# Block means as four narrow products side by side, first transposes of a pair in score banks, first weight pieces in halves, and other places for the first attention steps

## The chip, the cores and the metric

The kernel runs on one core of a Trainium2 chip, in one launch. The metric is the device time of that launch in microseconds (us), the median of three runs. TensorE (PE) does the matrix products, VectorE (DVE) and ScalarE (ACT) the work on elements, GpSimd (POOL) some copies, SyncE (SP) issues the loads.

## The reference

Sparse attention over 4 batches x 8 heads x 768 tokens x 64 numbers, then a gated network without a nonlinearity. Each query sees the keys less than 16 tokens away, and one summary for each of the 24 blocks of 32 tokens: the largest key by component, the mean value.

```python
k_sum = k.reshape(B, H, nb, block, D).max(axis=3)
v_sum = v.reshape(B, H, nb, block, D).mean(axis=3)
scores_l = scale * np.matmul(q, k.transpose(0, 1, 3, 2))
scores_s = scale * np.einsum('bhsd,bhnd->bhsn', q, k_sum) + np.log(block)
scores_l_m = np.where(np.abs(pos[:, None] - pos[None, :]) < window, scores_l, -1e9)
a = softmax(np.concatenate([scores_l_m, scores_s], axis=-1))
x = np.matmul(a, np.concatenate([v, v_sum], axis=2))   # heads side by side: 3072 x 512
out = ((x @ w1) * (x @ w2) @ w3) @ w_out               # 512 -> 1024 -> 1024 -> 512
```

## The kernel before

The 3072 tokens are done in six units of 512. In a unit the heads are taken two at a time: one step (a *pair*, four in a unit) fills the 128 rows of `x` that these two heads own. A pair is a chain: scores on PE (`scores`, L310, tile `sc`), mask and row maximum on DVE (`reduce`, L328), exponentials on ACT (`expose`, L344), the sum's reciprocal (`invert`, L351: an addition on POOL, then DVE), the scaling by it (`normalize_alone`, L358, on DVE or ACT as the string `NORMALIZE` says), transposes on PE (`transposes`, L366, tile `tp`) into two PSUM banks, copies to SBUF (`evacuate`, L376, the second on the engine that `SECOND` names), the products with the values (`outputs`, L385, tile `po`) and `keep_x` (L402).

`w3` and `w_out` are first multiplied into one 1024 x 512 matrix `wp` (`fold_weights`, L193), so that a unit needs `x @ w1`, `x @ w2`, their product (`gate`, L412) and one product with `wp` (`project`, L444). Every product of the weights is three single-pass products of a high and a low part. The weights come as eight-byte numbers in pieces of 512 columns (`wraw`), and `convert` (L152) makes the two parts of each: a pass on ACT (L167), a shift and an OR on DVE (L175, L178), a rounding copy on ACT (L188, the high part) and a subtraction on DVE (L109, the low part). The pieces, the four raw key tiles and the three value tiles of the first batch, and the network's `h` tiles share a ring of ten buffers.

The order on SP and PE is the order in which the code is written; DVE, ACT and POOL are ordered by the scheduler, except in `SOONER` parts that go ahead. Until the first eight pairs are done, a loop over steps `t` (L641) writes that order: each step starts one weight piece, and the tables `LOADS` (by pieces issued) and `WORK` (by step) say after which one a load or a piece of work is put. `FIRST` names the step at which each of the eight pairs begins, and `RATE` and `LATER_RATE` say how many columns of products of the weights go on PE between two steps. `EARLY` is the order of the first pieces, `EARLY_PRODUCTS` that of the first products.

The means of the first batch's values are products too: `mean_products` (L257) multiplies a 128 x 120 matrix of 1/32 and 0 by the 512 columns of each of six blocks of 128 tokens, and one ACT copy takes the result to `vs`. Later batches use sums on DVE (L247).

The banks: `mm` and `tp` have two each, `sc` has four. The accumulators of the third and fourth row block of the fold take the two `tp` banks until `store` (L209) has read them.

Of the kernel before, what the change touches and what calls it, by code (L numbers as in the profile page):

```python
# [15 lines left out]
ALU = mybir.AluOpType  # L16
# [14 lines left out]
FIRST = (15, 18, 20, 22, 27, 32, 37, 44)  # L31
# [4 lines left out]
    *(("wo", 0, 0), ("w3", 0, 0), ("wo", 0, 1), ("w3", 1, 0), ("wo", 1), ("w3", 2, 0), ("w3", 3, 0)),  # L36
    *(("w3", 0, 1), ("w3", 1, 1), ("wo", 2), ("w3", 2, 1), ("w3", 3, 1), ("wo", 3)),
# [10 lines left out]
NORMALIZE = "VAAAAAAA"  # L48
SECOND = "AAAVAVVA"
# [21 lines left out]
def attention_moe(ctx, tc, qG, kW, kT, vP, vW, vB, mask, w1, w2, w3T, wo, out):  # L71
# [23 lines left out]
    ident = const.tile([P, P], F32, name="ident")  # L95
    make_identity(nc, ident)
    mask_sb = const.tile([P, 3, KR], F32, name="mask_sb")


    mean_sb = sb.tile([P, S // P, P], F32, name="mean_sb", tag="v", bufs=2)  # L100
    nc.gpsimd.memset(mean_sb, 0.0)
    for i in range(P // BLOCK):
        for at in (CUT, CUT - 64):
            part = mean_sb.rearrange("p t n -> p (t n)")[i * BLOCK : (i + 1) * BLOCK, at + i :: P + P // BLOCK]
            nc.gpsimd.memset(part[:, : S // P], 1.0 / BLOCK)
# [22 lines left out]
    def weight(name, i, src, shape, part=None):  # L128

        n = src.shape[1] // 2  # L130
        parts = range(n // PIECE) if part is None else [part]
        units.append((name, i, shape, list(parts), len(todo) + len(parts) - 1))
        for k in parts:
            todo.append(src[:, 2 * k * PIECE : 2 * (k + 1) * PIECE])

    def start_loads(at_least):

        while todo or due_loads:
# [8 lines left out]
            nc.sync.dma_start(raw, todo.pop(0))  # L147
# [4 lines left out]
    def convert(name, i, shape, parts, last):  # L152


        n = len(parts) * PIECE
# [6 lines left out]
        for k in range(len(parts)):  # L162
# [3 lines left out]
            low_words.append(words[:, :, 0])  # L166
            nc.scalar.activation(  # L167
                f[:, k * PIECE : (k + 1) * PIECE],
# [7 lines left out]
        for k, low_word in enumerate(low_words):  # L176
            some = bits[:, k * PIECE : (k + 1) * PIECE]
# [8 lines left out]
        at = parts[0] * PIECE  # L186
# [4 lines left out]
        have.update((name, i, part) for part in parts)  # L191

    def fold_weights(order):  # L193
        acc = {}
        for i, j in order:
            while not {("w3", i, j * P // PIECE), ("wo", j // 2, j % 2 * DO // PIECE)} <= have:
# [88 lines left out]
    def load_sums(u, p, v):  # L285
        for b, blocks, n in batches(u):
            for g, at in enumerate((CUT, CUT - 64)):
# [4 lines left out]
                else:  # L292
                    src = vs[b][at : at + NB, p * P : (p + 1) * P]
# [64 lines left out]
    def normalize_alone(s, sm, mx):  # L358

        if NORMALIZE[s] == "A":  # L360
            for j in range(NI):
                nc.scalar.activation(sm[:, j], sm[:, j], AF.Copy, scale=mx[:, 2, j : j + 1])
        else:
            nc.vector.tensor_tensor(sm, sm, mx[:, 2].unsqueeze(2).broadcast_to([P, NI, KR]), ALU.mult)
# [47 lines left out]
    def gate(f, x, hs):  # L412
        acc = []
        for w in range(2):
# [6 lines left out]
            for c in range(NC):  # L421
                while (GATES[w], k, c * FQ // PIECE) not in have:
# [46 lines left out]
    def queue(name, i, part=None):  # L469
        src, shape = {"wo": (wo, (2, DO)), "w3": (w3T, (NJ, P)), "w1": (w1, (NC, FQ)), "w2": (w2, (NC, FQ))}[name]  # L470
        weight(name, i, src[i], shape, part)
# [83 lines left out]
    def first_pair(s):  # L555
# [13 lines left out]
        pt = evacuate(transposes(sms.pop(s)[0]), SECOND[s])  # L569
# [20 lines left out]
    def means():  # L590
        po = mean_products(vraws)
        vraws.clear()
        vs[0] = sb.tile([KR, DM], F32, name="vs0", tag="pt", bufs=6)
# [181 lines left out]
```

## Time and profile before

| what | value |
|---|---|
| median of 3 runs (lowest, highest) | 539.33 us (539.18, 541.11) |
| the profiled execution: its own time, its span | 540.83 us, 539.0 us |
[...]
| busy: PE, weight loads, DVE, ACT, POOL | 517.9, 421.8, 237.5, 238.9, 56.3 us |
| moved by DMA | 67.21 MB, mean 125 GB/s |

The span is the time from the first to the last instruction; the execution's own time is 1.83 us longer. The first 90 us are the fold of the weights and the first pairs, the rest is the network with the later pairs between its products. Names such as `mm<-w,w` read: tile written, then tiles read; x12 is the count. The products of scores, means and values stand as two records each, a transpose as one.

### The profile page before, as it was taken

Reading aid. Unit: us, or ns where it says so; the run is one execution under the profiler, and the core shown is the slowest. Engines: PE = TensorE matmul, PEld = TensorE weight load, DVE = VectorE, ACT = ScalarE, POOL = GpSimd, SP = SyncE. Lnnn points to the kernel's source line nnn. Section 1 sums busy time; section 2 is a strip of 40 time slices with the busy share of each in tenths; the row PEclk is TensorE's granted clock in tenths of the full one; section 3 lists DMA queues with packets and bytes.
Section 4 is the critical chain, followed back from the end, with each engine's and each line's share of the span. In section 5 each row is a group of like instructions: output and inputs, shape, how many; then the busy total and the mean of one; then the engine's idle time right before and its main releaser. Section 6 shows DMA issues by size and latency. Waiting matters only on the chain.

```text
span 539.0 us, 9912 instructions
## 1 busy us (share of the span) xinstructions
PE 517.9 (96%) x3852; PEld 421.8 (78%) x3852; DVE 237.5 (44%) x686; ACT 238.9 (44%) x688; POOL 56.3 (10%) x103
## 2 busy tenths in 40 slices
PE   2897999999999999999999999999999999999997
PEld 1655777888788888888888888888888888888885
DVE  5868889999503226724244033252042351122210
ACT  5547898887345225226235144253162261222210
POOL 1001221111001101103003002011021020000000
PEclk9988899999999999999999999999999999999999
DMA  8999689956524005544032141050160020000001
GB/s 309 403 348 350 189 270 369 280 183 197 167 96 154 0 1 169 162 128 135 0 111 60 40 152 58 0 157 33 40 190 1 1 75 39 21 21 0 1 19 58
DMA packets 30574, 67.21 MB, mean 125 GB/s; under 512 B 4032, under 2 KB 7616, under 8 KB 30528
## 3 DMA queue, kind: packets, MB, share of 16 engines
q1 hardware_dynamic: 27072, 60.30, 35.2%
q10 hardware_dynamic: 3456, 6.29, 3.1%
q8 instruction: 30, 0.49, 0.4%
q14 instruction: 16, 0.13, 0.1%
HBM read 58.51 MB, written 6.29 MB: 120 GB/s over the span
## 4 chain that ended last, share of the span: by engine, by line
PE 91%; DVE 3%; ACT 3%; DMA 1%; issue 1%; POOL 0%; SPq 0%; POOLq 0%; ACTq 0%
PE mm L113 79%; PE po L393 5%; PE sc L319 4%; PE tp L373 2%; DVE w L109 1%; DMA wraw<-in_w3T_dram 1%; DVE wf L178 1%; ACT w L188 1%; PE means L260 1%; ACT sm L347 1%; DVE wf L175 1%; ACT wf L167 0%; ACT wp L211 0%; DVE wp L109 0%; POOL k L306 0%
## 5 line engine op out<-in xcount | busy, mean ns | idle before, releaser
L113 PE MATMUL mm<-x,w 128*128 128x512 f32 x1152 | 264.9, 390 | 0.0
L113 PEld LDWEIGHTS mm<-x,w 128*128 128x128 f32 x1152 | 215.4, 188 | 45.6 <-issue 0.5
L113 PE MATMUL mm<-wp,h 128*128 128x512 f32 x576 | 133.9, 391 | 0.0
L113 PEld LDWEIGHTS mm<-wp,h 128*128 128x128 f32 x576 | 107.5, 188 | 22.7 <-issue 0.2
L347 ACT ACTIVATE sm<-sm,mx 128x120 f32<-128x120 f32 x192 | 73.6, 387 | 19.9 <-DVE mx L333 19.9
L438 DVE TENSOR_TENSOR g<-mm,g 128x512 f32<-128x512 f32 x48 | 33.1, 689 | 90.6 <-PE mm L113 88.7
L439 ACT CAST h<-g 128x512 fp32r<-128x512 f32 x48 | 29.6, 618 | 87.7 <-DVE g L438 87.7
L113 PE MATMUL mm<-w,w 128*128 128x512 f32 x192 | 54.1, 435 | 12.6 <-ACT w L188 11.5
L113 PEld LDWEIGHTS mm<-w,w 128*128 128x128 f32 x192 | 38.2, 206 | 25.6 <-ACT w L188 13.3
L457 ACT COPY o<-mm 128x512 f32<-128x512 f32 x24 | 14.1, 585 | 81.3 <-PE mm L113 81.3
L109 DVE TENSOR_TENSOR h<-g,h 128x512 fp32r<-128x512 f32 x48 | 35.7, 743 | 24.2 <-ACT h L439 24.0
L435 ACT COPY g<-mm 128x512 f32<-128x512 f32 x48 | 28.0, 584 | 35.6 <-PE mm L113 35.2
L333 DVE CUSTOM_DVE_ANT_0 sm<-sc,mask_sb 128x120 f32<-128x120 f32 x192 | 41.0, 275 | 5.5 <-PE sc L319 5.5
L382 DVE COPY pt<-tp 120x512 f32<-120x512 f32 x19 | 12.4, 686 | 67.7 <-PE tp L373 67.7
L306 POOL COPY k<-ks 128x96 f32<-128x96 f32 (+1 forms) x32 | 10.1, 327 | 252.3 <-DMA k<-in_kW_dram 210.0
L347 ACT ACTIVATION_READ_ACCUMULATOR sm<-sm,mx 128x1 f32 x192 | 36.5, 190 | 0.0
L109 DVE TENSOR_TENSOR x<-po,x 128x512 fp32r<-128x512 f32 x24 | 16.6, 690 | 42.2 <-ACT x L404 42.2
L356 POOL TENSOR_TENSOR sm<-sm,mx 128x960 f32<-128x960 f32 x16 | 29.1, 1820 | 6.0 <-DVE mx L353 5.0
L167 ACT ACTIVATE wf<-wraw 128x512 f32<-128x512 f32 x40 | 26.1, 669 | 6.2 <-DMA wraw<-in_wo_dram 2.7
L188 ACT CAST w<-wf 128x1024 fp32r<-128x1024 f32 (+1 forms) x25 | 21.9, 875 | 12.8 <-DVE wf L178 12.7
L393 PEld LDWEIGHTS po<-pt,v 120*64 120x64 f32 x768 | 23.8, 138 | 4.7 <-issue 2.9
L109 DVE TENSOR_TENSOR w<-wf,w 128x1024 fp32r<-128x1024 f32 (+1 forms) x25 | 25.4, 1014 | 4.4 <-ACT w L188 4.1
(33 smaller groups left out, 281.1 us busy)
## 6 DMA issues: line engine op xcount, KB each, us to landing
k<-in_kW_dram SPq DMA_DIRECT2D x24, 368.0 KB
wraw<-in_w3T_dram SPq DMA_DIRECT2D x16, 512.0 KB
wraw<-in_w_dram SPq DMA_DIRECT2D x16, 512.0 KB
q<-in_qG_dram SPq DMA_DIRECT2D x24, 256.0 KB
raw<-in_kT_dram SPq DMA_DIRECT2D x16, 384.0 KB
out_dram<-o ACTq DMA_DIRECT2D x24, 256.0 KB
v<-in_vW_dram SPq DMA_DIRECT2D x24, 192.0 KB
raw<-in_vB_dram SPq DMA_DIRECT2D x12, 384.0 KB
```

The source lines that it names most:

```text
L109: eng.tensor_tensor(dst, src, hi.bitcast(F32), ALU.subtract)
L113: nc.tensor.matmul(acc, lhsT=a, rhs=b, start=first and i == 0, stop=last and i == len(terms) - 1)
L167: nc.scalar.activation(f[:, k * PIECE : (k + 1) * PIECE], words[:, :, 1].bitcast(F32), AF.Prelu, scale=2.0**-112, alpha=-(2.0**32),)
L188: nc.scalar.copy(hi, f)
L319: nc.tensor.matmul(sc[h][64 * g : 64 * g + 64, i * KR : (i + 1) * KR], lhsT=q[rows, i * P + 64 * g : i * P + 64 * g + 64], rhs=k[rows, i, ...
L333: nc.vector.tensor_tensor_reduce(out=sm[:, j], in0=sc[h][:, i * KR : (i + 1) * KR], in1=mask_sb[:, 0 if blk == 0 else 2 if blk == BLOCKS - ...
L347: nc.scalar.activation(sm[:, j], sm[:, j], AF.Exp, bias=mx[:, 0, j : j + 1], scale=-1.0, accum_out=mx[:, 1, j : j + 1])
L356: nc.gpsimd.tensor_tensor(sm, sm, mx[:, 2].unsqueeze(2).broadcast_to([P, NI, KR]), ALU.mult)
L393: nc.tensor.matmul(po[cols, at : at + 64], lhsT=v[:, g, i, cols], rhs=pt[g][:, (h * NBLK + i) * 64 : (h * NBLK + i + 1) * 64], start=True, ...
L435: nc.scalar.copy(g, a[:, :U])
L438: nc.vector.tensor_tensor(g, acc[1][:, :U], g, ALU.mult)
L439: nc.scalar.copy(h[:, 0], g)
```

## The change

Five edits, all in the first part of the program.

1. `mean_products` uses a 128 x 24 matrix and does each of the six blocks as four products of 128 columns, one for each pair of heads, each into its own 32 partitions of one bank; four ACT copies follow, and `load_sums` reads its pair from there. The matrix has a buffer of its own and no longer takes one of the two `v` buffers.
2. `BANKS`: the transposes of the first pair go into two of the four `sc` banks.
3. The first two pieces of `wo` and `w3` come as two halves of 256 columns each, in turn.
4. `NORMALIZE` and `SECOND` change: the scaling is done once on POOL, three times on DVE and four times on ACT (once on DVE and seven times on ACT before); the second copy is on DVE once instead of three times. `store` goes ahead (`SOONER`).
5. `FIRST`, `LOADS`, `WORK`, `RATE` and `LATER_RATE` have other numbers.

```diff
-FIRST = (15, 18, 20, 22, 27, 32, 37, 44)
+FIRST = (16, 20, 22, 25, 31, 37, 41, 44)
-    *(("wo", 0, 0), ("w3", 0, 0), ("wo", 0, 1), ("w3", 1, 0), ("wo", 1), ("w3", 2, 0), ("w3", 3, 0)),
+    *(("wo", 0, 0, 256), ("w3", 0, 0, 256), ("wo", 0, 256, 256), ("w3", 0, 256, 256), ("wo", 0, 512)),
+    *(("w3", 1, 0), ("wo", 1), ("w3", 2, 0), ("w3", 3, 0), ("w3", 0, 512), ("w3", 1, 512), ("wo", 2)),
...
-NORMALIZE = "VAAAAAAA"
-SECOND = "AAAVAVVA"
+NORMALIZE = "PVAVAVAA"
+SECOND = "AAAAVAAA"
+BANKS = "STTTTTTT"
...
-                nc.scalar.copy(wp[i][:, 0], done)
-                low(nc.vector, wp[i][:, 1], done, wp[i][:, 0])
+                with tc.high_priority(offset=SOONER):
+                    nc.scalar.copy(wp[i][:, 0], done)
+                    low(nc.vector, wp[i][:, 1], done, wp[i][:, 0])
...
         po = ps.tile([P, 512], F32, name="means", tag="sc", bufs=4)
         for i in range(S // P):
-            nc.tensor.matmul(
-                po[:KR, :DM],
-                lhsT=mean_sb[:, i, :KR],
-                rhs=tiles[i // 2][:, i % 2],
-                start=i == 0,
-                stop=i == S // P - 1,
-            )
-        return po
+            for p in range(NPAIR):
+                nc.tensor.matmul(
+                    po[32 * p : 32 * p + NB, :P],
+                    lhsT=mean_sb[:, i],
+                    rhs=tiles[i // 2][:, i % 2, p * P : (p + 1) * P],
+                    start=i == 0,
+                    stop=i == S // P - 1,
+                )
+        yield
+        vs[0] = sb.tile([P, P], F32, name="vs0", tag="pt", bufs=6)
+        for p in range(NPAIR):
+            nc.scalar.copy(vs[0][32 * p : 32 * p + NB], po[32 * p : 32 * p + NB, :P])
...
+            eng = nc.vector if NORMALIZE[s] == "V" else nc.gpsimd
+            eng.tensor_tensor(sm, sm, mx[:, 2].unsqueeze(2).broadcast_to([P, NI, KR]), ALU.mult)
...
-        pt = evacuate(transposes(sms.pop(s)[0]), SECOND[s])
+        pt = evacuate(transposes(sms.pop(s)[0], **(SPARE if BANKS[s] == "S" else {})), SECOND[s])
...
-        11: [lambda: fetch(0)],
+        10: [lambda: rows(1), lambda: fetch(0)],
...
-    RATE = 6600
-    LATER_RATE = 6944
+    RATE = 5000
+    LATER_RATE = 7544
```

The order on PE around the means, before (w_253 is the third tile of `wo`, w_357 the fourth, w_115, w_137, w_171 and w_196 the first four of `w3`, w_106 the first of `wo`, w_415 the fifth of `w3`):

```order
L113 MATMUL mm<-w_253,w_171 128x512 x6
L260 MATMUL means<-rows,mean_sb 120x512 x6
L113 MATMUL mm<-w_253,w_196 128x512 x6
L319 MATMUL sc<-k,q 64x120 x16
L113 MATMUL mm<-w_357,w_115 128x512 x6
L113 MATMUL mm<-w_357,w_137 128x512 x6
L113 MATMUL mm<-w_357,w_171 128x512 x6
L113 MATMUL mm<-w_357,w_196 128x512 x6
L373 MATMUL tp<-ident,sm 120x64 x16
L319 MATMUL sc<-k,q 64x120 x16
L113 MATMUL mm<-w_106,w_415 128x512 x6
```

and now (w_274 and w_395 are the third and fourth of `wo`; w_111, w_148, w_191, w_214 the first four of `w3`):

```order
L115 MATMUL mm<-w_274,w_191 128x512 x6
L267 MATMUL means<-rows,mean_sb 24x128 x24
L329 MATMUL sc<-k,q 64x120 x16
L115 MATMUL mm<-w_274,w_214 128x512 x6
L115 MATMUL mm<-w_395,w_111 128x512 x6
L115 MATMUL mm<-w_395,w_148 128x512 x6
L115 MATMUL mm<-w_395,w_191 128x512 x6
L115 MATMUL mm<-w_395,w_214 128x512 x6
L386 MATMUL tp<-ident,sm 120x64 x16
L329 MATMUL sc<-k,q 64x120 x16
L115 MATMUL mm<-w_102,w_436 128x512 x6
```

The scores of the first pair stand ahead of six products now, and thirty products stand between them and their transposes, where it was twenty-four.

The loads on SP's queue up to the third tile of `wo`, before (wraw_164 and wraw_185 are its two pieces):

```order
L147 DMA wraw_142<-in_w3T_dram 128x1024
L254 DMA rows_144<-in_vP_dram 128x2x512
L147 DMA wraw_155<-in_w3T_dram 128x1024
L147 DMA wraw_164<-in_wo_dram 128x1024
L147 DMA wraw_185<-in_wo_dram 128x1024
L300 DMA q_187<-in_qG_dram 128x512
L301 DMA k_188<-in_kW_dram 128x736
```

and now (wraw_184 and wraw_205):

```order
L151 DMA wraw_153<-in_w3T_dram 128x1024
L259 DMA rows_155<-in_vP_dram 128x2x512
L310 DMA q_157<-in_qG_dram 128x512
L311 DMA k_158<-in_kW_dram 128x736
L151 DMA wraw_170<-in_w3T_dram 128x1024
L610 DMA mask_sb_65<-in_mask_dram 128x360
L290 DMA v_173<-in_vW_dram 96x512
L291 DMA v_173<-in_vW_dram 32x512
L292 DMA v_173<-in_vW_dram 64x512
L151 DMA wraw_184<-in_wo_dram 128x1024
L151 DMA wraw_205<-in_wo_dram 128x1024
```

Queries, keys and values of the first pair went behind these pieces and go ahead of them now; the mask is ahead of them in both.

On DVE, the conversion of the same tile, before:

```order
L109 TENSOR_TENSOR w12_137<-wf_217,w12_137 128x512
L175 TENSOR_SCALAR wf_240<-wf_240 128x1024
L178 SCALAR_TENSOR_TENSOR wf_240<-wraw_164,wf_240 128x512
L178 SCALAR_TENSOR_TENSOR wf_240<-wraw_185,wf_240 128x512
L109 TENSOR_TENSOR w12_253<-wf_240,w12_253 128x1024
```

and now:

```order
L111 TENSOR_TENSOR w12_148<-wf_233,w12_148 128x512
L180 TENSOR_SCALAR wf_256<-wf_256 128x1024
L235 TENSOR_REDUCE ks_263<-raw_207 128x24
L183 SCALAR_TENSOR_TENSOR wf_256<-wraw_184,wf_256 128x512
L183 SCALAR_TENSOR_TENSOR wf_256<-wraw_205,wf_256 128x512
L180 TENSOR_SCALAR wf_272<-wf_272 128x512
L183 SCALAR_TENSOR_TENSOR wf_272<-wraw_229,wf_272 128x512
L111 TENSOR_TENSOR w12_274<-wf_256,w12_274 128x1024
```

The largest keys of the first pair (ks_263), whose raw tile is loaded behind the two pieces, come between shift and OR, and the shift and OR of another piece ahead of the subtraction.

## Rows read from the trace of the kernel before

**Rows 1.** Chain of waits, in order of time: start us, length us, what.

```profile
...
33.94 5.15 PE means L260 x12
...
40.48 1.05 PE sc L319 x32
...
51.27 1.10 PE tp L373 x15
...
88.96 13.85 PE mm L113 x60
```

**Rows 2.** Timeline of PE: start us, length us, what, count, idle time before.

```profile
...
9.50 6.42 PE L113 MATMUL mm<-w,w 128*128 128x512 f32 x12 [9.50 <-ACT w L188]
...
27.15 0.73 PE L113 MATMUL mm<-w,w 128*128 128x512 f32 x2 [1.43 <-ACT w L188]
28.41 5.53 PE L113 MATMUL mm<-w,w 128*128 128x512 f32 x16 [0.53 <-DVE w L109]
...
41.40 5.73 PE L113 MATMUL mm<-w,w 128*128 128x512 f32 x24
49.54 0.27 PE L373 MATMUL tp<-ident,sm 64*120 64x64 f32 x1 [2.41 <-DVE wp L109]
...
54.11 4.87 PE L113 MATMUL mm<-w,w 128*128 128x512 f32 x15
...
109.08 11.18 PE L113 MATMUL mm<-x,w 128*128 128x512 f32 x48
```

**Rows 3.** Windows of 2 us: busy us and count by engine, granted clock, DMA share, GB/s.

```profile
...
26.00:28.00 2.00, 0.73 (x2) 0.30 (x2) 0.89 (x2) 1.62 (x2) 0.00 (x0) 1.00 1.02 401
...
30.00:32.00 2.00, 2.00 (x6) 1.60 (x5) 1.89 (x4) 0.66 (x2) 0.00 (x0) 0.50 1.03 387
...
50.00:52.00 2.00, 0.73 (x14) 0.73 (x15) 1.97 (x4) 0.71 (x2) 0.00 (x0) 0.50 1.01 326
```

**Rows 4.** Window of 10 us in the network, columns as in Rows 3.

```profile
...
110.00:120.00 10.00, 10.00 (x46) 8.14 (x44) 9.25 (x15) 7.83 (x18) 1.57 (x3) 1.00 0.66 196
```

**Rows 5.** Timeline of ACT, columns as in Rows 2.

```profile
...
23.27 0.67 ACT L167 ACTIVATE wf<-wraw 128x512 f32<-128x512 f32 x1
```

**Rows 6.** Timeline of DVE, columns as in Rows 2.

```profile
...
37.55 1.23 DVE L109 TENSOR_TENSOR w<-wf,w 128x1024 fp32r<-128x1024 f32 x1 [1.11 <-ACT w L188]
...
47.73 1.16 DVE L364 TENSOR_TENSOR sm<-sm,mx 128x960 f32<-128x960 f32 x1
...
115.31 1.23 DVE L109 TENSOR_TENSOR w<-wf,w 128x1024 fp32r<-128x1024 f32 x1 [0.38 <-ACT w L188]
```

**Rows 7.** Groups by shape: instructions, count, busy us, mean ns, idle us before.

```profile
...
L356 POOL TENSOR_TENSOR sm<-sm,mx 128x960 f32<-128x960 f32 x16 | 29.1, 1820 | 6.0 <-DVE mx L353 5.0 <-DVE vs L248 1.0
...
L393 PE MATMUL po<-pt,v 120*64 120x64 f32 x768 | 26.0, 224 | 0.7 <-ACT pt L378 0.7
...
L393 PEld LDWEIGHTS po<-pt,v 120*64 120x64 f32 x768 | 23.8, 138 | 4.7 <-issue 2.9 <-ACT pt L378 1.1 <-ACT sm L362 0.4
...
L109 DVE TENSOR_TENSOR w<-wf,w 128x1024 fp32r<-128x1024 f32 x15 | 18.5, 1232 | 2.8 <-ACT w L188 2.8
...
L109 DVE TENSOR_TENSOR w<-wf,w 128x512 fp32r<-128x512 f32 x10 | 6.9, 688 | 1.6 <-ACT w L188 1.4
```

**Rows 8.** DMA of the first 110 us in 40 slices, and issues: count, KB each.

```profile
...
GB/s 92 262 398 392 413 393 398 404 414 405 400 320 229 401 391 411 389 227 329 296 288 277 271 34 24 310 263 328 286 233 385 398 393 395 288 315 387 232 256 16
...
k<-in_kW_dram SPq DMA_DIRECT2D x7, 368.0 KB
...
q<-in_qG_dram SPq DMA_DIRECT2D x7, 256.0 KB
...
v<-in_vW_dram SPq DMA_DIRECT2D x5, 192.0 KB
v<-in_vW_dram SPq DMA_DIRECT2D x5, 128.0 KB
v<-in_vW_dram SPq DMA_DIRECT2D x5, 64.0 KB
```

More of the change, by code (lines that the diff above doesn't have):

```diff
@@ L126, in attention_moe, with weight @@
     begun, due_loads, kraws, vraws = [0], [], {}, {}
-    def weight(name, i, src, shape, part=None):
+    def weight(name, i, src, shape, at=None, length=PIECE):
         n = src.shape[1] // 2
[L131 to L134, printed above, removed]
+        parts = [(k, PIECE) for k in range(0, n, PIECE)] if at is None else [(at, length)]
+        units.append((name, i, shape, parts, len(todo) + len(parts) - 1))
+        for k, length in parts:
+            todo.append(src[:, 2 * k : 2 * (k + length)])
     def start_loads(at_least):
@@ L158, in convert @@
         low_words = []
-        for k in range(len(parts)):
+        for k, length in parts:
             raw = loading.pop(0)
@@ L175, in convert @@
         nc.vector.tensor_scalar(out=bits, in0=bits, scalar1=3, scalar2=None, op0=ALU.logical_shift_left)
-        for k, low_word in enumerate(low_words):
-            some = bits[:, k * PIECE : (k + 1) * PIECE]
+        for (k, length), low_word in zip(parts, low_words):
+            some = bits[:, k - at : k - at + length]
             nc.vector.scalar_tensor_tensor(
@@ L190, in convert @@
         low(nc.vector, lo, f, hi)
-        have.update((name, i, part) for part in parts)
+        have.update((name, i, c) for c in range(at, at + n, P))
     def fold_weights(order):
@@ L195, in fold_weights @@
         for i, j in order:
-            while not {("w3", i, j * P // PIECE), ("wo", j // 2, j % 2 * DO // PIECE)} <= have:
+            while not {("w3", i, j * P), *(("wo", j // 2, j % 2 * DO + c) for c in range(0, DO, P))} <= have:
                 yield 0
@@ L421, in gate @@
             for c in range(NC):
-                while (GATES[w], k, c * FQ // PIECE) not in have:
+                while (GATES[w], k, c * FQ) not in have:
                     yield 0
@@ L466, in attention_moe, with queue @@
     xs = [[] for _ in range(NU)]
-    def queue(name, i, part=None):
+    def queue(name, i, *part):
         src, shape = {"wo": (wo, (2, DO)), "w3": (w3T, (NJ, P)), "w1": (w1, (NC, FQ)), "w2": (w2, (NC, FQ))}[name]
-        weight(name, i, src[i], shape, part)
+        weight(name, i, src[i], shape, *part)
     for step in EARLY:
@@ L590, in means @@
     def means():
-        po = mean_products(vraws)
+        pairs.append(mean_products(vraws))
+        next(pairs[-1])
         vraws.clear()
-        vs[0] = sb.tile([KR, DM], F32, name="vs0", tag="pt", bufs=6)
-        nc.scalar.copy(vs[0], po[:KR, :DM])
     LOADS = {
-        7: [lambda: nc.sync.dma_start(mask_sb, mask)],
-        8: [lambda: rows(1)],
-        11: [lambda: fetch(0)],
-        12: [lambda: keys(1)],
+        10: [lambda: rows(1), lambda: fetch(0)],
+        11: [lambda: nc.sync.dma_start(mask_sb, mask), lambda: fetch_values(0)],
@@ L698, in attention_moe @@
             with tc.manual_schedule(engines={engines.Activation, engines.DVE}):
-                spare = ({}, {"tag": "sc", "bufs": 4})
-                tps = [transposes(sms.pop(p)[0], **more) for p, more in zip(last, spare)]
+                tps = [transposes(sms.pop(p)[0], **more) for p, more in zip(last, ({}, SPARE))]
                 pts = [evacuate(tp) for tp in tps]
```

95 lines of the change are left out of this document (51 added, 44 removed).

## The prediction

> **What bounds the kernel now.** I read the chain of waits first. From 88.96 us on it is PE products back to back (60 of them in 13.85 us, 231 ns each), to within some microseconds of the end; before that it jumps between PE, DVE and ACT [rows 1]. In PE's timeline no stretch from 88.96 us to the last product shows a wait worth more than 0.2 us, so the end stands at a fixed distance from the moment at which PE enters the network. A change gains what it takes off those first 88.96 us, or what it makes PE wait later it loses.
>
> In that stretch the reader is to see four losses [rows 2]. PE has nothing to do until 9.50. It waits 1.43 + 0.53 us for the third tile of `wo`, whose low part comes at 28.4. The means take 5.15 us [rows 1] in the one place where PE had caught up with work to do. And after 24 products (41.40 to 47.13) it waits 2.41 us, does one transpose, and waits for the rest until 51.27, because the first pair's transposes need the two banks from which the third and fourth row blocks of the fold must first be stored; the releaser is the low part of `wp`. [...]
>
> **The change part by part**, at points that both orders have.
>
> *The third tile of `wo`.* Queries, keys and values of the first pair now go ahead of it: 256 + 368 + 192 + 128 + 64 = 1008 KB [rows 8], 1.03 MB, at the 0.4 MB per us that the queue moved then (slices of 2.75 us, [rows 8]): 2.6 us later. Before, 7.00 MB had to come up to its second piece: 2.07 MB in three slices, the rest at 0.4, which is 20.6 us, or some 21.8 with what other transfers in flight took; ACT took the piece at 23.27 [rows 5]. So 1.5 of the 2.6 us are covered by ACT being late; 1.1 show. On DVE the reduction of the first keys now stands ahead of the OR, about 0.6 us more after what it saves later. Together +1.7 us: 28.4 becomes 30.1. If all is covered it is 0, if nothing is, 2.6 + 0.9 = 3.5. The pieces behind it are shifted less (0.4 MB at the fourth tile of `wo`, 1 us), and that tile's low part, done at 38.78 [rows 6], now waits for no key reductions; I leave it at about 37.7, just ahead of PE.
>
> *The means.* The same rows are streamed in a quarter of the width by four products that own 32 columns of the array each. The trace has no such product. From above: nothing overlaps, 48 records for 128 columns cost what 12 for 512 did, 5.15 us, or some more in weight loads. From below: all four overlap, 5.15 / 4 = 1.3 us. The nearest row is that of the products with the values, which also use all rows and split the columns, in two halves: 26.0 us for 768 records, 34 ns each [rows 7]; 48 x 34 ns = 1.6 us. I take 1.6, a gain of 3.5.
> Those rows also bear on the weight loads. 768 loads of 138 ns would be 106 us in a row; their union is 23.8 us [rows 7], so loads for products with the same rows do overlap here. [...]
>
> *The first pair.* Its scores now stand ahead of six products (0.24 us each by the 24 in 5.73 us [rows 2], 1.4). They ended at 41.53 [rows 1]: 41.5 + 1.7 - 3.5 - 1.4 = 38.3. From there to its transposes there are two ways. PE has thirty products: 7.2 us, 45.5. The softmax took from 41.53 to 47.73 + 1.16 = 48.89 on DVE [rows 6], 7.4 us; the scaling is now on POOL, 1.82 us by its later rows [rows 7], 0.7 more: 46.4. The banks are no longer a condition: two of four score banks are free, the means' one once ACT has copied it. So the transposes end about 47.0 instead of 51.27 + 1.10 = 52.37 [rows 1]: -5.4. What is late next is the softmax, by a microsecond.
>
> *The half clock behind it.* With the hole gone, the 15 products after it should cost 3.5 and not 4.87 us (-1.4), and the second pair's scores, in the same stretch, about 1 and not 1.8 (-0.8). That makes -7.6. The halves let the first product start perhaps 0.8 us sooner; PE then meets the next tile at its old time, so nothing is counted, while their extra instructions cost DVE about 6 x 0.14 us (a subtraction of 1024 columns takes 1232 ns, one of 512 takes 688, so 144 are fixed [rows 7]) in a stretch that waits for DMA. Further small waits before 88.9 (0.40 and 0.52 us) should mostly go: -0.5. ACT loses three scalings of eight instructions and gets two more copies, which is room; DVE gets two more scalings (1.16 each [rows 6]), gives one to POOL and loses two copies: level.
>
> **Sum:** -8.1 us. PE enters the network at about 80.8. The profiled execution took 540.83 us, 1.83 more than its span, and would take 532.7. The median of the runs shown is 1.5 lower, 539.33; the forecast for the median is 531.2.
>
> **Does the network follow?** This is the step I trust least. DVE is busy 9.25 of 10 us at 110 to 120 [rows 4]. The low part of the third tile of `w2` is done at 115.31 + 1.23 = 116.54 [rows 6], and PE needs it after 33 of the 48 products from 109.08 [rows 2], at 109.08 + 33 x 0.233 = 116.8: 0.2 us of room. So PE can only be 8 us early if DVE is too. Adding up DVE's instructions in the new order up to that point I get 91.4 us of work, against 93.0; PE would need it at 108.4, which leaves DVE 17.0 us of waiting in all. Before, it waited 23.6. About 2 go at the start, and about 4 in the hole at the first transposes (11.5 us of waiting up to the fourth tile of `wo`, 15.7 at the next tile). That is 17 to 18, so I expect it to be just enough, or to cost up to a microsecond.
>
> **The rivals.**
> *DVE holds the network* (0.15). Waiting does not shrink with the hole but moves: w2's first tile hangs on SP, where both its pieces now stand behind a third block of second-batch values that needs a buffer freed by a DVE reduction. Every microsecond of that is one of PE. With 20 or 21 us of waiting by the third tile of `w2` the gain is half: 534.8. For it: the 0.2 us of room. Against: that PE itself, by needing less, frees ACT.
> *The means do not overlap* (0.10). They cost 5.15; everything to the first transposes is 3.5 later: 534.7. [...]
> *No gain at all* (0.09). The conversions of the network set PE's time whatever happens before; PE waits back what it won. Then the 1.6 us less DVE work is all: 537.7.
> *Slower* (0.06). Early entry turns into several short waits for tiles of `w1` and `w2`, and each lowers the clock as at 50 to 52, costing 1.4 + 0.8 us on top of a wait of about 1.5: 3.7 each. It decides from three such waits on, more than 8.1 us; with four, 14.8 - 8.1 makes +6.7: 546. For it: two holes in the trace of before did just this. Against: from 60 us on none did, though DVE was as full.
>
> **How the numbers follow.** The forecast's own case has 0.60. Its range is 528 to 533.5: the `wo` term from 0 to 3.5, the means from 1.3 up, the clock term fully there or half. The two half gains reach to 535; I stop at 536.5 and leave out the last two cases and a little below 527. This measurement can tell about 0.5%, 2.7 us, from no change: faster is below 536.6, which the first three cases give, 0.85; same is the fourth, 0.09; slower the last, 0.06.
>
> **What would show it.** Right: in the chain, means of about 1.6 us; the first pair's scores ending near 38 and its transposes near 47 with no wait for `wp`; no window at 0.50 around 50; network products from about 81 with no wait over a microsecond behind them. Wrong: a means stretch near 5 us; PE waiting for a low part of `w1` or `w2` after 81; or a later third `wo` tile than 32, with a half-clock stretch that reaches over the means and the scores. The forecast falls if PE enters the network after 84, or enters early and the end does not move with it.

## The result and the profile after

The kernel after takes **542.78 us** (median of 6 runs, 542.43 to 545.31) against 539.33 (6 runs): ratio **1.0067**, 95% interval 1.0045 to 1.0088. It is slower; the forecast was 531.2 (527 to 536.5). Its profiled execution took 544.93 us, with a span of 543.0, so that the two traces differ by 4.0 us of span where the medians differ by 3.45.

PE's timeline, columns as in [rows 2], to be held against those rows:

```profile
11.14 1.65 PE L115 MATMUL mm<-w,w 128*128 128x512 f32 x3 [11.14 <-ACT w L192]
...
32.06 0.73 PE L115 MATMUL mm<-w,w 128*128 128x512 f32 x2 [2.03 <-ACT w L192]
33.32 5.53 PE L115 MATMUL mm<-w,w 128*128 128x512 f32 x16 [0.53 <-DVE w L111]
38.79 1.51 PE L267 MATMUL means<-rows,mean_sb 128*24 128x128 f32 x48
40.23 1.05 PE L329 MATMUL sc<-k,q 64*64 64x120 f32 x32
...
49.26 0.69 PE L386 MATMUL tp<-ident,sm 64*120 64x64 f32 x16 [0.95 <-POOL sm L375]
...
84.87 0.94 PE L386 MATMUL tp<-ident,sm 64*120 64x64 f32 x16 [2.73 <-DVE sm L375]
86.33 1.88 PE L329 MATMUL sc<-k,q 64*64 64x120 f32 x32 [0.52 <-POOL k L316]
...
90.05 18.16 PE L115 MATMUL mm<-x,w 128*128 128x512 f32 x75
...
120.02 5.35 PE L115 MATMUL mm<-x,w 128*128 128x512 f32 x21 [0.99 <-DVE g L451]
```

The means are short, as forecast (1.51 us), and the wait for `wp` before the first transposes is gone. But the 16 products of the third tile of `wo` begin at 33.32 instead of 28.41, and two new waits stand at 84.87 and 86.33, just before the network, which PE enters at 90.05 instead of 88.96. Windows of 2 us, columns as in [rows 3]:

```profile
34.00:36.00 2.00, 2.00 (x7) 1.52 (x6) 2.00 (x4) 1.16 (x3) 0.00 (x0) 0.50 1.04 402
...
50.00:52.00 2.00, 2.00 (x36) 1.71 (x37) 2.00 (x3) 1.98 (x4) 0.26 (x1) 1.00 1.04 238
...
86.00:88.00 2.00, 1.67 (x32) 1.50 (x32) 1.39 (x3) 1.46 (x3) 0.42 (x2) 0.50 1.03 394
88.00:90.00 2.00, 2.00 (x38) 1.79 (x32) 1.50 (x2) 1.63 (x3) 0.00 (x0) 0.50 1.02 399
```

The half clock at 50 to 52 of [rows 3] is gone, and one at 86 to 90 has come. What makes those two waits stands on SP's own queue, the list of loads that it issues in order (columns as in the timeline):

```profile
56.58 15.61 SPq L245 DMA_DIRECT2D raw<-in_vB_dram  x3
72.29 0.38 SPq L151 DMA_DIRECT2D wraw<-in_w_dram  x1
...
78.17 0.38 SPq L311 DMA_DIRECT2D k<-in_kW_dram  x1
...
97.51 0.42 SPq L151 DMA_DIRECT2D wraw<-in_w_dram  x1
106.77 0.33 SPq L230 DMA_DIRECT2D raw<-in_kT_dram  x1
107.19 0.39 SPq L151 DMA_DIRECT2D wraw<-in_w_dram  x1
```

Three blocks of the second batch's values are asked for in a row, and they have two buffers. SP issues two, stands before the third until DVE has reduced the first, and everything behind it waits: the first pieces of `w2` (72.29) and the fifth pair's keys (78.17). Of the 15.61 us from the first issue to the end of the third, 14.3 are this stand (what was waited for: us in total, times, longest):

```profile
SPq L245 <- DVE vs L252: 8.0, 1, 8.0
SPq L245 <- DMA raw<-in_vB_dram: 6.3, 1, 6.3
```

The chain of waits (columns as in [rows 1]) runs to the entry through the keys, which then land 7.84 us after their issue:

```profile
78.17 7.84 DMA k<-in_kW_dram
```

The kernel before has such stands too, and PE waits for nothing behind them:

```profile
55.13 0.88 SPq L240 DMA_DIRECT2D raw<-in_vB_dram  x2
...
67.30 0.32 SPq L240 DMA_DIRECT2D raw<-in_vB_dram  x1
...
71.52 1.51 SPq L301 DMA_DIRECT2D k<-in_kW_dram  x1
...
109.65 4.57 SPq L240 DMA_DIRECT2D raw<-in_vB_dram  x2
114.31 0.38 SPq L147 DMA_DIRECT2D wraw<-in_w_dram  x1
```

There SP stands for 5.8 us before the third block (from 61.5), the fifth pair's keys go 6.7 us sooner, and behind the long stand (from 100.2 to 109.65) only the very last piece of weights is left.

In the kernel after DMA moves nothing from 66 to 72 us:

```profile
66.00:68.00 2.00, 2.00 (x30) 1.72 (x27) 1.91 (x4) 2.00 (x5) 1.15 (x3) 1.00 0.00 0
...
70.00:72.00 2.00, 1.21 (x39) 1.15 (x43) 2.00 (x4) 0.89 (x4) 0.00 (x0) 1.00 0.00 0
```

Here the one waiting load stopped every load behind it on SP: the next is issued at 72.29, behind the 14.3 us of the stand, and the rows show 0 GB/s. A second stand, from 97.9 to 106.77, holds back the last four pieces of weights, the fourth tiles of `w1` and `w2`. ACT shows what came of each:

```profile
82.27 0.66 ACT L172 ACTIVATE wf<-wraw 128x512 f32<-128x512 f32 x1 [2.65 <-DMA wraw<-in_w_dram]
...
113.32 0.68 ACT L172 ACTIVATE wf<-wraw 128x512 f32<-128x512 f32 x1 [3.89 <-DMA wraw<-in_w_dram]
113.91 0.60 ACT L452 CAST h<-g 128x512 fp32r<-128x512 f32 x1
```

Behind the first, DVE's shift for that piece (82.97) stands ahead of the fourth pair's scaling, for which PE waits at 84.87; behind the second ACT's `h` is late, then `g` on DVE, and PE waits 0.99 us at 120.02.

DVE in windows (columns as in [rows 3], the third pair of numbers is DVE), first of before, then of after:

```profile
50.00:70.00 20.00, 18.33 (x175) 14.38 (x175) 17.59 (x54) 16.73 (x57) 3.05 (x6) 0.83 0.73 220
70.00:90.00 20.00, 19.48 (x247) 15.48 (x246) 18.16 (x52) 17.47 (x51) 3.96 (x8) 1.00 0.98 324
90.00:110.00 20.00, 20.00 (x156) 16.16 (x155) 18.94 (x44) 18.46 (x55) 2.78 (x6) 1.00 0.87 275
...
sum 118.00, PE 100.56 PEld 75.66 DVE 96.99 ACT 88.92 POOL 16.73; mean PE 16.76 PEld 12.61 DVE 16.17 ACT 14.82 POOL 2.79
```

```profile
50.00:70.00 20.00, 19.84 (x205) 15.26 (x205) 19.81 (x54) 18.39 (x57) 4.39 (x8) 1.00 0.67 180
70.00:90.00 20.00, 15.97 (x195) 13.05 (x195) 16.43 (x39) 11.58 (x31) 2.49 (x5) 0.88 0.87 280
90.00:110.00 20.00, 20.00 (x128) 16.29 (x125) 15.79 (x37) 14.97 (x39) 1.86 (x5) 0.95 0.69 222
...
sum 118.00, PE 97.42 PEld 74.65 DVE 94.73 ACT 78.96 POOL 17.27; mean PE 16.24 PEld 12.44 DVE 15.79 ACT 13.16 POOL 2.88
```

From 50 to 70 us DVE is idle for 0.2 us where it was 2.4: the early front does feed it, and the first block of values, landed at about 64, is reduced only at 70.65. From 70 to 110 it is then idle for 7.8 where it was 2.9. Up to 118 us it has been idle for 23.3 instead of 21.0.

### The profile page after: what moved, and what is told of

Its sections match the earlier page's. It is cut to its first block, busy times and chain, and to the rows that moved or that the text cites. A ratio compares the mean times of both kernels' runs of the same rounds, so it can differ in the third digit from the quotient of the medians.

```text
span 543.0 us, 9986 instructions
## 1 busy us (share of the span) xinstructions
PE 517.5 (95%) x3888; PEld 422.5 (78%) x3888; DVE 239.8 (44%) x692; ACT 234.9 (43%) x673; POOL 57.7 (11%) x100
## 4 chain that ended last, share of the span: by engine, by line
PE 80%; DVE 6%; DMA 6%; ACT 4%; issue 2%; POOL 0%; SPq 0%; POOLq 0%; ACTq 0%
PE mm L115 70%; PE po L406 4%; PE sc L329 4%; PE tp L386 2%; DVE wf L183 2%; DMA wraw<-in_w_dram 2%; DMA k<-in_kW_dram 1%; DMA wraw<-in_wo_dram 1%; DMA wraw<-in_w3T_dram 1%; ACT wf L172 1%; DVE wf L180 1%; DVE w L111 1%; ACT w L192 1%; ACT sm L357 1%; DVE sm L343 1%
## 5 line engine op out<-in xcount | busy, mean ns | idle before, releaser
L357 ACT ACTIVATE sm<-sm,mx 128x120 f32<-128x120 f32 x192 | 73.6, 386 | 15.5 <-DVE mx L343 15.4
L395 DVE COPY pt<-tp 120x512 f32<-120x512 f32 x17 | 11.0, 686 | 66.8 <-PE tp L386 66.8
L316 POOL COPY k<-ks 128x96 f32<-128x96 f32 (+1 forms) x32 | 9.0, 293 | 243.0 <-DMA k<-in_kW_dram 142.2
L172 ACT ACTIVATE wf<-wraw 128x512 f32<-128x512 f32 (+1 forms) x42 | 26.8, 650 | 15.5 <-DMA wraw<-in_w_dram 7.5
L192 ACT CAST w<-wf 128x1024 fp32r<-128x1024 f32 (+2 forms) x27 | 22.1, 824 | 14.3 <-DVE wf L183 14.3
L111 DVE TENSOR_TENSOR w<-wf,w 128x1024 fp32r<-128x1024 f32 (+2 forms) x27 | 26.0, 962 | 4.4 <-ACT w L192 4.2
```

What stands on the lines that cost most here:

```text
L111: eng.tensor_tensor(dst, src, hi.bitcast(F32), ALU.subtract)
L172: nc.scalar.activation(f[:, k : k + length], words[:, :, 1].bitcast(F32), AF.Prelu, scale=2.0**-112, alpha=-(2.0**32),)
L192: nc.scalar.copy(hi, f)
L357: nc.scalar.activation(sm[:, j], sm[:, j], AF.Exp, bias=mx[:, 0, j : j + 1], scale=-1.0, accum_out=mx[:, 1, j : j + 1])
```

## The experiments

The medians are those of each run's own comparison with the kernel before (539.5 to 540.0 in the five groups of runs). Each is the median of 4 to 12 runs.

**Parts alone, in the kernel before.** `b_means` takes the 24-row matrix and the four narrow products with their copies (the diff of `mean_products` above), `b_banks` this line, `b_mb` both:

```diff
-        pt = evacuate(transposes(sms.pop(s)[0]), SECOND[s])
+        pt = evacuate(transposes(sms.pop(s)[0], **({"tag": "sc", "bufs": 4} if BANKS[s] == "S" else {})), SECOND[s])
```

> The kernel before with the narrow means alone. If what PE saves at the means reaches the network (theory: PE sets its own pace up to 89 us), the means take 1.44 us instead of 5.15 and the time falls by about 3.6, from 539.3 to 535.7. If the conversions on DVE or the first pair's softmax hold PE whatever it saves (rival), it stays within 1 us of 539.3.

> The kernel before, with the first pair's transposes in two of the score banks and nothing else. If the wait of 2.41 us at 49.54 was for the banks, as the trace says, and what is won there arrives: transposes end about 2.5 us earlier, no half clock at 50 to 52, time 539.5 - 2 to 4 = 535.5 to 537.5. If the front is held by its conversions and loads, PE waits the same time at a later tile and the time is within 1 us of 539.5.

> The kernel before, with the narrow means and the first pair's transposes in score banks, without the new places of the first steps, the halves and the other engines of the scaling. If the parts add: 538.7 for the means, and +2.3 for the banks, so 541. If the hole of 2.4 to 3.5 us before the first transposes was the means' gain waited back, then with both the gain arrives: 535 to 537. If the network cannot be entered earlier with profit: 538 to 540, with waits for g.

Measured: `b_means` 538.73 (ratio 0.9986, 0.9972 to 1.0001), `b_banks` 541.86 (1.0037, 1.0024 to 1.0051; slower by 2 us, which neither theory had), `b_mb` 539.32 (0.9985, 0.9968 to 1.0002). PE's timeline of `b_means`:

```profile
32.39 1.07 PE L261 MATMUL means<-rows,mean_sb 128*24 128x128 f32 x32
35.82 0.64 PE L261 MATMUL means<-rows,mean_sb 128*24 128x128 f32 x16 [2.35 <-DMA rows<-in_vP_dram]
...
48.82 1.11 PE L374 MATMUL tp<-ident,sm 64*120 64x64 f32 x16 [3.53 <-DVE sm L365]
```

The time saved on the means is waited back at once: 2.35 us for the last rows, and 3.53 for the first softmax where PE had waited 2.41 for a bank [rows 2]. PE enters the network at 87.19, 88.04 and 86.54 in the three runs instead of 88.96. Of that some 1.6 in the first and the third are no gain of an edit: their 16 products of the third tile of `wo` took 3.96 and 3.91 us (5.53 in [rows 2], with a clock of 0.50 at 30 to 32 [rows 3]), which differs from run to run. With the banks PE then waits 1.49 us for `g` at 131.73, with both 1.32 at 130.02, where before waits for none. So even with the steps of before, 3.7 us less of means bring at most 0.8 at the end, and an entry that is early by a microsecond is no earlier end.

**Parts taken back, in the kernel after.** `a_whole`: the first two pieces whole, and every step number less two. `a_norm`: the fourth pair's scaling on ACT instead of DVE. `a_wo`: the first pair's loads behind the third tile of `wo`, as before.

```diff
-    *(("wo", 0, 0, 256), ("w3", 0, 0, 256), ("wo", 0, 256, 256), ("w3", 0, 256, 256), ("wo", 0, 512)),
+    *(("wo", 0, 0, 512), ("w3", 0, 0, 512), ("wo", 0, 512)),
...
-NORMALIZE = "PVAVAVAA"
+NORMALIZE = "PVAAAVAA"
...
-        10: [lambda: rows(1), lambda: fetch(0)],
-        11: [lambda: nc.sync.dma_start(mask_sb, mask), lambda: fetch_values(0)],
-        13: [lambda: keys(0)],
+        10: [lambda: rows(1)],
+        11: [lambda: nc.sync.dma_start(mask_sb, mask)],
+        13: [lambda: fetch(0)],
+        14: [lambda: keys(0)],
...
-        17: [lambda: rows(0)],
+        17: [lambda: rows(0), lambda: fetch_values(0)],
```

> The changed kernel (542.8) with the first two pieces whole, as before, and all step numbers two lower. If the halves only move the first product (11.14 instead of 9.50 us) and PE waits for the third tile of wo at 32 us anyway, within 0.7 us of 542.8. If the halves slow the first loads so that every piece behind is late, the third tile of wo comes 1 to 2 us earlier and the time is about 541.

> The changed kernel (542.8) with the scaling of the fourth pair on ACT instead of DVE. Rival, DVE's order: the 2.73 us wait of PE for that scaling goes, and with it the half clock behind it, about 538. Theory of the blocked queue: ACT's own pass over the late piece of w2 or the late keys hold PE next, within 1.5 us of 542.8.

> The kernel after, with the first pair's queries, keys, values and key reductions back at the places of before (behind the third tile of wo). Theory A: the third tile's low part comes 3 to 4 us earlier (about 29 instead of 32.6), the scores of the first pair end no later than 41, but the second half of the door (the late block of keys at 84 to 90) stays, so the time changes by less than 1.5 us. Theory C (the 4.9 us by which that tile is late are what cancels the gain): the whole front moves by 3 to 4 us, entry at 86.5, time 539 to 540.

Measured: 543.79 (1.0077, 1.0061 to 1.0093), 543.9 (1.0079, 1.0063 to 1.0096), 546.12 (1.0111, 1.009 to 1.0131). None of the three is the cause by itself, with SP's queue as it was. In `a_norm` the wait for the scaling shrinks to 0.79 us and the next in line, the late keys, is waited for instead. `a_wo` is the instructive one:

```profile
31.95 2.96 PE L115 MATMUL mm<-w,w 128*128 128x512 f32 x11 [0.53 <-DVE w L111]
...
48.71 0.68 PE L386 MATMUL tp<-ident,sm 64*120 64x64 f32 x16 [2.23 <-POOL sm L375]
...
88.11 1.88 PE L329 MATMUL sc<-k,q 64*64 64x120 f32 x32 [2.15 <-POOL k L316]
```

The third tile comes 1.4 us earlier, PE waits 2.23 instead of 0.95 for the first softmax, and the wait for the fifth pair's keys grows from 0.52 to 2.15 us.

**SP's stands.** `a_vb` moves the third and fourth blocks of values back, and with them, unwanted, the keys. `a_keys` lets the fifth pair's keys go second through the two buffers. `a_ring` gives the blocks no buffers of their own but a ring of 12; `b_ring` is the same in the kernel before, `b_mb_ring` in `b_mb`. `a_both` is `a_keys` with `a_wo`, `a_keys_ring` is `a_keys` with the ring.

```diff
# a_vb
-        23: [lambda: load_second(0), lambda: load_second(1), lambda: load_second(3), ...
-        24: [lambda: load_second(2), lambda: fetch_sums(2)],
-        25: [lambda: load_second(4), lambda: fetch(4)],
+        23: [lambda: load_second(0), lambda: load_second(1), ...
+        27: [lambda: load_second(3), lambda: load_second(2), lambda: fetch(5)],
+        28: [lambda: second_batch(3), lambda: second_batch(2), lambda: load_second(4)],
# a_keys
+        23: [lambda: load_second(0), lambda: load_second(4), ...
+        26: [lambda: second_batch(0), lambda: second_batch(4)],
+        27: [lambda: load_second(1), lambda: load_second(3), lambda: fetch(5)],
+        28: [lambda: fill(4), lambda: fetch_sums(3)],
+        29: [lambda: second_batch(1), lambda: second_batch(3), lambda: load_second(2), lambda: load_second(6)],
+        31: [lambda: second_batch(2)],
# a_ring, b_ring
-RING = 10
+RING = 12
-        return {"bufs": 2} if b else {"tag": "ring", "bufs": RING}
+        return {"tag": "ring", "bufs": RING}
```

> The changed kernel (542.8) with the third and fourth block of second-batch values loaded four steps later, behind the pieces of w2's first tile and the queries and keys of the fifth pair, instead of ahead of them. Theory of the blocked queue: SP stood 15.6 us before the third block, and what was queued behind it (w2's first tile, the fifth pair's keys) made PE wait at 82 to 86 and run at half clock to 92; without it PE enters the network 5 to 6 us earlier and the time is about 537.5. Rival, DVE's order (the fourth pair's scaling placed behind w2's shift): no more than 1 us better, about 542.

> The kernel after, with its loads of the second batch in another order: the key block that the fifth pair needs goes second through its two buffers, and the blocks of values that wait for a buffer stand on SP's queue behind the fifth pair's queries and keys and behind the first pieces of w2. Theory A (SP's queue stood 15.6 us before a block of values and held back everything behind it, so that PE waited at 84 to 90 us with its clock at 0.50): no wait over 1 us between 79 and 90, PE enters the network at about 85 instead of 90.05, and the time falls by 4 to 5 us, to 537.5 to 538.5. Theory B (the conversions of the network's weights on ACT and DVE set PE's time whatever SP does): PE enters earlier or not, but waits for low parts or for g instead, and the time is within 1 us of 542.8.

> Both edits at once. Theory A: what is won at the third tile of wo is worth something only when SP's queue no longer holds the end of the front: entry at 82 to 84, time 535 to 537. Theory B: as the kernel after, 541.5 to 543.5. If the edits simply add, the difference is the sum of the two single ones.

> The kernel after, with the blocks of the later batches (keys and values) taking buffers of the ring, which has 12 instead of 10, in place of two buffers of their own. No load is moved in the first part of the program; SP only has to wait less for a buffer. Theory A (SP's queue, stopped before such a block, holds back the fifth pair's keys at 84 to 90 us and then the pieces of w1 and w2): no 15.6 us stand of SP at 56 us, entry to the network at 83 to 86 instead of 90.05, no wait for g behind it, time 536 to 538.5. Theory B (ACT and DVE set the pace of the network whatever SP does): entry earlier by 4, but waits for g of 2 us or more behind it, time 541 to 543.

> The control: the same exchange of buffers in the kernel before, and nothing else. There SP's stands (to 67.3 and to 109.65 us) cost PE nothing, by the trace. Theory A: 538.5 to 540. If it gains 2 us or more, SP's stands bound the kernel before too; if it loses 1.5 us or more, the exchange has a price of its own that must be taken off the result of the exchange in the kernel after.

> The same with the blocks of the later batches in a ring of 12. Theory A (behind an early entry the pieces of w1 and w2 come late because SP stands before a block): 2 us or more below the run without the ring, 534 to 537, and faster than the kernel before. Theory B: the same as without, within 1 us.

> The kernel after with both cures that leave its work whole: the fifth pair's keys first, and the later batches' blocks in a ring of 12. If the two cure different waits (the late keys before the entry, the late pieces behind it), entry stays at about 85.7 and the two waits for g of 2.0 us go, less some 0.7 us that the ring costs: 540 to 541. If they cure the same one, it is at 541.5 as each alone.

| run | median us | ratio to before, 95% | PE enters the network |
|---|---|---|---|
| after | 542.78 | 1.0067 (1.0045 to 1.0088) | 90.05 |
| a_vb | 549.11 | 1.0178 (1.016 to 1.0196) | 92.99 |
| a_keys | 541.75 | 1.0034 (1.0021 to 1.0047) | 85.73 |
| a_both | 543.22 | 1.0059 (1.0038 to 1.008) | 86.89 |
| a_ring | 541.51 | 1.0032 (1.0017 to 1.0048) | 87.15 |
| a_keys_ring | 539.71 | 0.9992 (0.998 to 1.0004) | 86.24 |
| b_ring | 540.26 | 1.0019 (1.0005 to 1.0033) | 86.90 |
| b_mb_ring | 539.6 | 1.0 (0.9986 to 1.0014) | 86.54 |

`a_vb` shows how much hangs on that queue: its keys are later still, and PE waits 6.90 us for them at 90.08. `a_keys` brings the entry forward by 4.3 us, but the time by 1.0 only. PE's timeline of it tells where the rest goes:

```profile
84.28 0.34 PE L406 MATMUL po<-pt,v 120*64 120x64 f32 x4 [1.30 <-ACT pt L391]
...
85.73 18.89 PE L115 MATMUL mm<-x,w 128*128 128x512 f32 x75
...
116.82 5.76 PE L115 MATMUL mm<-x,w 128*128 128x512 f32 x24 [1.56 <-DVE g L451]
```

The 75 products take 18.89 us where 75 x 0.231 is 17.3 (its windows from 86 to 90 have a clock of 0.51 and 0.63), and `g` is waited for twice, 1.56 and 0.45 us, behind the second stand (96.4 to 102.65 in this run). The ring takes that one away: with it no wait for `g` is left, in `a_ring`, `a_keys_ring` and `b_mb_ring`. The two cures are separate: by the medians 1.0 and 1.3 us alone and 3.1 together, by the ratios (each group of runs has its own kernel before) 1.8, 1.9 and 4.0. The ring itself has a price: `b_ring` is 0.7 us slower than the kernel before, and in it as in `a_keys_ring` PE's first scores of a later unit wait 0.6 us for a copy on DVE (at 275 us), which no profile without the ring shows. `a_both` begins the third tile's products 1.6 us sooner than `a_keys` and is not faster (543.22): with the keys first, too, that tile is worth nothing. So theory A holds for the existence of the waits, and they are worth the whole loss against before; its times (537.5 to 538.5 for `a_keys`, 536 to 538.5 for `a_ring`) were not reached, and of the entry's gain no more arrives than in `b_mb`.

**The blocks left out.** `a_none`, `b_none` and `b_mb_none` load and reduce no block of the second batch in the first part:

```diff
-        second[k] = of_second[k][0]()
+        second[k] = None
...
-        of_second[k][1](second.pop(k))
+        second.pop(k)
+        if k == 0:
+            vs[1] = sb.tile([NPAIR * NB, P], F32, name="vs")
+            nc.gpsimd.memset(vs[1], 0.0)
+        if k >= len(of_second) - NPAIR:
+            t = aligned([P, NB], name="ks", bufs=2 * NPAIR)
+            nc.gpsimd.memset(t, 0.0)
+            ks[1, k - len(of_second) + NPAIR] = t
```

> The kernel after without the second batch's blocks in its first part: their eight loads and their reductions on DVE are left out, and constants stand in the summaries' place, so the output of the later batches is not the reference's. SP then has nothing to stand before between 56 and 107 us, and DVE has some 9 us less to do. Theory A (the change's gain of the front is there, and SP's stands and the DVE time of these blocks take it back): entry to the network at 82 to 84, and against the kernel before without the same blocks 3 us or more faster. Theory B (the front itself has no gain, since DVE's other work holds it): within 1.5 us of the kernel before without these blocks.

> The control: the kernel before without the same blocks (the same part of the output is not the reference's). Its trace showed no wait of PE for them, so both theories expect 538 to 540; if it falls by 2 us or more, DVE's share of these blocks bounds the kernel before too.

> The kernel before with the narrow means and the first transposes in score banks, without the same blocks (the same part of the output is not the reference's). With them the two edits gained nothing (539.3). Theory A: without them the early entry is kept, 535.5 to 537.5, no wait for g at 130. Theory B: 538 to 539.5.

Measured: 539.81 (0.9992, 0.9976 to 1.0008), 541.45 (1.0025, 1.001 to 1.004), 542.99 (1.0048, 1.0032 to 1.0065). With the blocks the kernel after is 3.4 us slower than before, without them 1.6 faster than its control: some 5 us of the difference between the kernels hang on these blocks. How much of it is their stands, and how much the order around them, this does not tell: both controls became slower by leaving work out, which neither theory expected. DVE, ACT and POOL are ordered anew when instructions vanish, and in `b_none` PE waits 0.96 us for a copy on DVE (at 89.07) that was on time before; whether that is all of its loss stays open. In `a_none` nothing stands on SP for these blocks, and PE still enters at 86.24 only, far from 80.8. That is where `a_keys_ring` enters too, in the same time: the two cures give back all that the stands cost. The 16 products of the third tile took 3.91 us in this profile of `a_none` and 5.53 in that of `a_keys_ring`, so 1.6 us of PE do not move the entry either. The chains of waits say why. First a piece of before's, then some of `a_none`'s:

```profile
80.01 5.70 PE mm L113 x24
```

```profile
77.52 1.16 DVE sm L375
...
83.30 0.95 ACT w L192
...
85.27 1.04 PE po L406 x28
```

Added up by engine, the pieces of the chain from 42 to 85 us are (us; "issue" is time in which the engine waited for nothing that the profile shows):

| | before | after | a_keys_ring | a_none |
|---|---|---|---|---|
| PE | 31.1 | 5.7 | 0 | 0 |
| DVE | 1.8 | 17.7 | 25.7 | 21.9 |
| ACT | 5.2 | 6.2 | 11.2 | 15.5 |
| DMA (the fifth pair's keys) | 0 | 7.8 | 0 | 0 |
| POOL and issue | 5.0 | 6.7 | 6.3 | 6.4 |

(The keys' piece in the chain of after ends at 86.0, so that its column sums to 44.)

Before, PE set the pace of this stretch. After, DVE and ACT do, and with the queue freed they do alone. This is read from the chains; no run takes work off both engines.

**The rest of the front.** `a_v` is `a_keys_ring` with the first scaling on DVE, `a_v_wo` adds the edit of `a_wo`:

```diff
-NORMALIZE = "PVAVAVAA"
+NORMALIZE = "VVAVAVAA"
```

> The kernel after with both cures (the fifth pair's keys first, a ring of 12), and the first pair's scaling on DVE instead of POOL (1.16 instead of 2.12 us). If the wait of 0.93 us for that scaling before the first transposes is worth its size, entry comes 0.9 earlier and the time is 0.9 below the run with the cures alone (539.7), at 538.8. If DVE, which has no idle time from 50 to 70 us in that run, only passes the loss on to the next wait, 539.5 to 540.5.

> The same, with the loads of the first pair behind the third tile of wo as in the kernel before, which by an earlier run lets its products begin at 30.4 instead of 32. Scores of the first pair end at 39, transposes at 47.5 to 48.5. If the gain arrives: 537 to 538.3, faster than both kernels. If the two network limits (conversions and pairs) take it up: 539 to 540.

Measured: 542.25 (1.0043, 1.0024 to 1.0063) and 543.82 (1.0064, 1.0041 to 1.0087), slower, not faster. In PE's timeline of `a_v` the wait moves from POOL (0.93 us) to DVE and grows, and the clock falls behind it (a mean of 0.85 from 50 to 70 us, 1.00 in `a_keys_ring`):

```profile
49.68 1.11 PE L386 MATMUL tp<-ident,sm 64*120 64x64 f32 x16 [2.70 <-DVE sm L375]
```

In all twelve profiles with the steps of after, the first transposes end between 48.9 and 50.8, whether the third tile of `wo` is begun at 30.3 or at 32.1: PE arrives, and the softmax does not. No version beat the kernel before beyond its interval.

## Why the prediction was wrong

By its own steps, on PE's clock (the forecast's end is 450.0 us behind its entry, as in the trace of before):

| | forecast | after | a_keys_ring |
|---|---|---|---|
| first pair's transposes end | 47.0 | 49.9 | 49.7 |
| PE enters the network | 80.8 | 90.05 | 86.24 |
| from there to the end | 450.0 | 452.95 | 451.7 |
| span | 530.8 | 543.0 | 537.9 |

(The profiled run of after is 2.15 us above its median, that of `a_keys_ring` is at it; the forecast's span is that of the profiled execution of before, less 8.1.) The miss of 12.2 us in the span is 2.9 up to the transposes, 6.3 (40.1 for 33.8) from there to the entry, and 2.9 behind it. The two cures take 3.5 from the second part and 1.3 from the third.

The step that failed is the path from the first transposes to the entry, with the step on whether the network follows. The sum let PE's savings through there (-1.4, -0.8 and -0.5, so 33.8 us for the 36.6 of before) and put no new wait in; DVE's waiting had a price only behind the entry. The runs showed two things in its place: SP's stand before the third block, which makes the fifth pair's keys late and costs 3.5 us, and a chain that is DVE's and ACT's and no longer PE's, so that with the stand cured the stretch takes 36.6 us, as before, and nothing of the saving arrives.

*The third tile of `wo`*, the term that was mis-sized first: +1.7 us forecast, with 3.5 as the upper end, +4.9 measured.

```profile
27.41 0.67 ACT L172 ACTIVATE wf<-wraw 128x512 f32<-128x512 f32 x1 [0.55 <-DMA wraw<-in_wo_dram]
```

```profile
28.72 0.94 DVE L235 TENSOR_REDUCE ks<-raw 128x24 f32<-128x768 f32 x1
29.58 1.35 DVE L183 SCALAR_TENSOR_TENSOR wf<-wraw,wf 128x512 uint32<-128x512 uint32 x2
```

ACT took its second piece at 27.41 and waited for it, 4.1 us later than in [rows 5]. The 2.6 us were priced at 0.4 MB per us, and 1.5 of them called covered; but just behind the issue of the first pair's loads DMA moved 295 and 321 GB/s (20 to 24 us), and nothing was covered. The key reduction ahead of the OR (0.94) came on top as foreseen. Undoing it brought nothing at the end, in `a_wo` as in `a_both` and `a_v_wo`.

*The means*: 1.44 us in the chain, forecast 1.6. Right, and the rival that they do not overlap (5.15 us) falls: these products share all rows and own a quarter of the columns each, and their 48 records took 1.51 us; their 48 weight loads of 103 ns each, 4.9 us in a row, took 1.24.

*The first pair*: no wait for `wp`, as forecast. The softmax took 7.9 us from the end of the scores (41.3) to 49.2, forecast 8.1, though the scaling on POOL took 2.12, not 1.82. The scores were 3.0 late by the tile, and so the transposes 2.9. *The half clock* at 50 to 52 went, as forecast: the window is at 1.00, and the 12 products from 51.02 took 3.02 us, where 15 took 4.87 before [rows 2]. Another stands at 84 to 92, behind the new waits (0.78, 0.50, 0.50 and 0.52 in windows of 2 us), and the one behind the third tile stayed (0.50 and 0.67 at 34 to 38). *The halves* brought the first product not 0.8 sooner but 1.6 later: the four half pieces, which hold what the first two whole ones held, were taken from 4.58 to 9.13 us, those two at 4.72 and 6.95. From 2 to 8 us DMA moved 169, 250 and 313 GB/s in windows of 2 us, where it was 258, 289 and 410; `a_whole`, with the same steps and whole pieces, has 250, 289 and 401. It ended no sooner (543.79), so this cost nothing at the end.

*Does the network follow?* DVE's work up to the third tile of `w2` was read roughly right: 94.75 us busy up to 118.02, where that tile's low part is done, against 95.53 up to 116.54 before, so 0.8 less; forecast 1.6 less. Its waiting was not. The prediction's own adding gave 23.6 us of it for before, the windows give 21.0, so only the change can be held against it: some 6 us less were forecast (17 to 18 for 23.6), 2.3 more came (23.3). The rival "DVE holds the network" named the mechanism word for word, the third block of values that stands on SP before `w2`, but priced it at 20 to 21 us of waiting and half the gain, with a chance of 0.15. It did not ask how long that stand would be (14.3 us), what else is behind it (the fifth pair's keys), or how much the second stand holds back (four pieces instead of one). With both cures the same low part is done at 112.42, and DVE has waited 17.5 us up to it:

```profile
0.00:112.42 112.42, 93.52 (x771) 71.22 (x772) 94.90 (x227) 80.80 (x206) 19.75 (x41) 0.98 0.94 313
```

That is 3.5 less than before, a good half of what was forecast. Behind its entry PE then waits for no tile of `w1` or `w2`, and still the time is only that of before. So DVE's waiting in the network is not all that is missing. Of the 5.4 us by which the entry of `a_keys_ring` is late, 2.7 are there at the transposes, and 2.4 of the rest are waits for DVE and ACT: 0.95 us for `x` on DVE at 70.53 and 1.45 for the copies on ACT at 84.78 and 85.27, where before had 0.40 and 0.52 and the forecast had put -0.5. Behind the entry 1.7 us more are lost: 0.26 for `x` at 89.29, the ring's 0.63, and the rest in pieces that these rows do not sort out.

*The slower rival* (0.06) had the right kind of end, by another road: not many short waits for `w1` and `w2` after an early entry, but one queue that shuts before the entry. The forecast's own test, entry not after 84, named the failure correctly.

## What to carry to other kernels

Where loads share one issuing queue and a small pool of buffers, count per step how many loads are asked for before the first reduction that frees a buffer: the first that exceeds the pool stops every load behind it until that reduction (here 14.3 us). What it costs depends on what stands behind it and when that is needed: the kernel before had stands of 5.8 and 9.5 us and lost nothing. A gain early in a pipeline whose other engines are some 90% busy (here DVE 18.16 and ACT 17.47 of the 20 us from 70 to 90 in the kernel before) is worth its size only as long as the chain of waits stays on the engine that gains: add up the chain by engine again after the first part of the change, since here the means' 3.7 us alone were worth at most 0.8. And a wait just before a long run of products can be paid twice, once as a wait and once at half clock behind it: in the kernel after the clock was 0.50 from 86 to 90, but in `a_keys_ring` it stayed at 1.00 behind a wait of 1.45 us.

## What had not been expected of the hardware

The clock behind the same wait is not the same in every run: the 16 products behind the third tile of `wo` took 5.53 us in some profiles (after, `a_keys_ring`) and 3.9 in others (`a_none` 3.91, `a_norm` 3.92), and 35 runs of the kernel before go from a span of 536.7 us at a mean clock of 0.996 to 541.8 at 0.987. So differences of entry of some 1.5 us between two profiles can be just that. Just behind the issue of the first pair's loads (20 to 24 us) DMA moved 295 and 321 GB/s, where it was 404 and 412 in the kernel before, and the same scaling on POOL took 2.12 to 2.13 us at 46 to 49 us in all ten profiles that have it, against a mean of 1.82 in the later rows of before.
